# One plan slot sooner and the last store on another queue: attention products of a fused kernel on one core

## Chip, cores, metric

One Trainium2 chip, one core of it. The metric is device time in microseconds (us), the median of several executions. Executions can fall into a slower state, at a lower granted TensorE clock. Times inside a trace are us from the start of the profiled execution's span.

## The reference

A block-wise linear attention with decay (batch 4, 8 heads, 768 tokens, head width 64), followed by a bilinear feed-forward layer over 3072 tokens of width 512:

```python
for b in range(nb):                        # blocks of a sequence
    intra = np.einsum('bhic,bhjc->bhij', qb, kb) * Dmask[None]
    intra = np.einsum('bhij,bhjd->bhid', intra, vb)
    inter = np.einsum('bhid,bhde->bhie', qb * lam_pow[None], kv_state)
    out[:, :, sl] = intra + inter
    kv_state = lam_block[None, :, None, None] * kv_state + np.einsum('bhsd,bhse->bhde', kb_dec, vb)
...
a = x @ w_a; b = x @ w_b                   # 3072x512 by 512x1536
return (a * b @ w_out).astype(np.float32)
```

## The kernel before

Tokens come in 24 units of 128; the feed-forward layer runs over groups of units (`GROUPS = (4, 1, 2, 4, 4, 4, 4, 1)`). While a group's feed-forward products keep TensorE busy, a fixed plan slips the attention work of later units between them. A plan entry is (slot, piece, unit), where a slot is a place after one step of the group's products; entries with the same slot run in the order of the list.

```python
PLAN = {
    0: [(0, "V", 3), (8, "C", 0), ... (30, "PV", 4), (34, "O", 4),        # cut
        (35, "PK", 5), (35, "PV", 5)],
    ...
    2: [(0, "V", 6), (1, "T", 7), (1, "P", 8), (4, "T", 8), (4, "P", 9), (6, "S", 7),
        (6, "S", 8), (7, "V", 7), (6, "P", 10), (10, "V", 8), ...],       # cut
}
```

Pieces: O are a unit's attention products with the cast of their result to xT (ACT); S are scores (TensorE) and two mask products (VectorE, L330); V is the state update: `kvd` products on TensorE (L369), then a copy of the state on VectorE (L401), for which the next unit's `kvd` must wait, because they add to the same bank; P prepares a unit: two scaling products on GpSimd (L262 for k, L267 for q) and a cast of v to bf16 (L276).

```python
def prep_v(u):
    make_vb(u, "pool" if u < n0 + 3 else "dve")     # n0 = 4: from unit 7 on VectorE
    pump()                                           # issues the next loads
def kv_copy(u, ps, eng="dve"):
    ...
    nc.vector.tensor_mul(st..., ps..., bdiag_bc)     # L401; ps is a PSUM bank
...
def store(row, op, lo, hi):
    if row < g_u0[KEEP_GROUPS]:
        ...                                          # o_kept: ACT copy now, stored later
        return
    o_sb = o_pool.tile([128, d_model], F32, name="o_sb", tag="osb")
    nc.scalar.copy(o_sb[:, lo:hi], op[:, lo:hi])                       # L467
    nc.sync.dma_start(out=out_r[row][:, lo:hi], in_=o_sb[:, lo:hi])    # L468
...
            if last and t == n - 1:                  # the last unit, in three column parts
                for lo, hi in ((0, 256), (256, 384), (384, 512)):
                    ...
                    store(u0 + t, op, lo, hi)
```

Of the kernel before, what the change touches and what calls it, by code (L numbers as in the profile page):

```python
# [22 lines left out]
def _bc(ap, dims):  # L23
# [17 lines left out]

PLAN = {
    0: [(0, "V", 3), (8, "C", 0), (9, "C", 1), (15, "C", 2), (18, "C", 3), (23, "PK", 4),
        (26, "C", 4), (26, "T", 4), (29, "C", 5), (29, "S", 4), (30, "PV", 4), (34, "O", 4),
        (35, "PK", 5), (35, "PV", 5)],
    1: [(0, "V", 4), (2, "T", 5), (3, "PK", 6), (6, "PV", 6), (6, "S", 5), (7, "T", 6),
        (10, "S", 6), (12, "O2", (5, 6)), (13, "P", 7)],
# [18 lines left out]
def kernel(  # L66
# [11 lines left out]
    nc = tc.nc  # L78
    B, H, S, D = q.shape
# [3 lines left out]
    d_model, d_ff = moe_w_a.shape  # L83
# [25 lines left out]
    def ps_bank(name, shape, dt, hold=False, ffn=False, at=None):  # L109
        i = bank["next"] if at is None else at  # L110
        while i in bank["held"] or (ffn and i == bank["ffn"]):
            i = (i + 1) % 7
        if ffn:
            bank["ffn"] = i
        bank["next"] = (i + 1) % 7
        if hold:
            bank["held"].add(i)
        return ps_pool.tile(shape, dt, name=name, tag=f"ps{i}")
# [34 lines left out]
    def cast_w(kind, c, eng):  # L153
        t = staged.pop((kind, c))
        if kind == "o":
            dst = wo_sb[:, 2 * c:2 * c + 2, :]
        else:
            dst = (wa_sb if kind == "a" else wb_sb)[:, :, w_off[c]:w_off[c + 1]]
        if eng == "act":
            nc.scalar.copy(dst, t)  # L160
        elif eng == "pool":
            nc.gpsimd.tensor_copy(dst[:, :, :128], t[:, :, :128])
            nc.gpsimd.tensor_copy(dst[:, :, 128:], t[:, :, 128:])
        else:
            nc.vector.tensor_copy(dst, t)  # L165
        pump()
# [39 lines left out]
    for w, src in (("q", q), ("k", k)):  # L206
        x4_r = src[0, :, 0:PACK * BLK, :].rearrange("h (p r) d -> p h (r d)", r=PACK)
        n_h = 4 if w == "q" else 2
        for h in range(0, H, n_h):
            t = wst_pool.tile([128, 1024], F32, name=w + "4", tag="wst")[:, :n_h * 256]  # L210
            nc.sync.dma_start(out=t.rearrange("p (h x) -> p h x", h=n_h), in_=x4_r[:, h:h + n_h])
            t = t.rearrange("p (h r d) -> p h r d", h=n_h, r=PACK)
# [220 lines left out]
    out_r = out.rearrange("(t p) n -> t p n", p=128)  # L433
# [10 lines left out]
    def a_part(f, xT, gt, cuts=None):  # L444
        ps = half(wa_sb, f, xT, gt, "a_ps", cuts)
        a_sb = a_pool.tile([128, 512], BF16, name="a_sb", tag="a")
        nc.scalar.copy(a_sb[:, :gt], ps[:, :gt])  # L447
        return a_sb

    def b_part(f, xT, gt, a_sb, ab):  # L450
        ps = half(wb_sb, f, xT, gt, "b_ps")
        nc.vector.tensor_mul(ab[:, f, :gt], a_sb[:, :gt], ps[:, :gt])  # L452
# [4 lines left out]
        row, o_sb = kept.pop(0)  # L457
        nc.sync.dma_start(out=out_r[row], in_=o_sb)

    def store(row, op, lo, hi):  # L460
        if row < g_u0[KEEP_GROUPS]:
            o_sb = wst_pool.tile([128, 1024], F32, name="o_kept", tag="wst")[:, :d_model]
            nc.scalar.copy(o_sb, op)
            kept.append((row, o_sb))
            return
        o_sb = o_pool.tile([128, d_model], F32, name="o_sb", tag="osb")
        nc.scalar.copy(o_sb[:, lo:hi], op[:, lo:hi])  # L467
        nc.sync.dma_start(out=out_r[row][:, lo:hi], in_=o_sb[:, lo:hi])  # L468

    def out_mms(op, ab, t, fs, lo=0, hi=d_model):  # L470
        for f in fs:
            nc.tensor.matmul(op[:, lo:hi], lhsT=ab[:, f, t * 128:(t + 1) * 128],  # L472
                             rhs=wo_sb[:, f, lo:hi], start=(f == 0), stop=(f == FC - 1))

    def ffn(u0, n, xT, hook, first, last):
        gt = n * BLK
        ab = ab_pool.tile([128, FC, 512], BF16, name="ab", tag="ab")
        if first:
            for i, cs in enumerate(W_STEPS):
                nxt = W_STEPS[i + 1][0] if i + 1 < len(W_STEPS) else None  # L480
                fs = range(w_off[cs[0]] // 128, w_off[cs[-1] + 1] // 128)
                a_sbs = [a_part(f, xT, gt, ((0, gt - BLK), (gt - BLK, gt)) if f == 0 else None)
                         for f in fs]
                if i == 0:
                    cast_w("b", cs[1], "act")
                elif nxt:
                    cast_w("a", nxt, "dve")
                for n_f, (f, a_sb) in enumerate(zip(fs, a_sbs)):
                    b_part(f, xT, gt, a_sb, ab)
                    hook(f)  # L490
                    if i == 0 and n_f == 1:
                        cast_w("a", nxt, "dve")
                if nxt:
                    cast_w("b", nxt, "act")
            ops = [ps_bank("op", [128, d_model], F32, hold=True) for _ in range(n)]
            slot = FC
            for c in range(FC // 2):
                for t in range(n):
                    out_mms(ops[t], ab, t, range(2 * c, 2 * c + 2))
                    if c == FC // 2 - 1:  # L500
                        store(u0 + t, ops[t], 0, d_model)
                    hook(slot)
                    slot += 1
            bank["held"].clear()
            return
        for f in range(FC):
            a_sb = a_part(f, xT, gt)
            b_part(f, xT, gt, a_sb, ab)
            hook(f)
        for t in range(n):  # L510
            op = ps_bank("op", [128, d_model], F32, ffn=True)
            if last and t == n - 1:
                for lo, hi in ((0, 256), (256, 384), (384, 512)):
                    if lo:
                        op = ps_bank("op", [128, d_model], F32, ffn=True)
                    out_mms(op, ab, t, range(FC), lo, hi)
                    store(u0 + t, op, lo, hi)
                return
            out_mms(op, ab, t, range(FC // 2))
            hook(FC + 2 * t)  # L520
            out_mms(op, ab, t, range(FC // 2, FC))
            store(u0 + t, op, 0, d_model)
            hook(FC + 2 * t + 1)
# [135 lines left out]
    for g, n in enumerate(GROUPS):  # L659
# [6 lines left out]
        def hook(slot, plan=plan):  # L666
            for name, us in plan.get(slot, ()):
                if name == "C":
                    cast_w("o", us, "dve")
                elif name == "PK":  # L670
                    prep_k(us)
                elif name == "PV":
                    prep_v(us)
                elif name == "P":
                    prep_k(us)
                    prep_v(us)
                elif name == "W":
                    store_kept()
                elif name == "T":
                    piece_T(us)  # L680
                elif name == "S":
                    piece_S(us)
                elif name == "V":
                    piece_V(us)
                elif name == "O":
                    pieces_O((us,))
                elif name == "O2":
                    pieces_O(us)
                else:
                    pieces_O(us[:2], us[2:])  # L690

        ffn(g_u0[g], n, gx.pop(g), hook, g == 0, g + 1 == len(GROUPS))

# [28 lines left out]
```

## Time and profile before

| | before |
|---|---|
| time, first 3 runs | 233.46 us (233.22 to 233.78) |
| span of the profiled run | 231.5 us |
| TensorE / VectorE / ACT / GpSimd busy | 97% / 50% / 39% / 22% of the span |
| loss of TensorE's stream before the second group's first product | 0.34 us |
| end of the last ACT copy to the end of the span | 3.08 us |

TensorE is the bound: an engine other than TensorE matters only where TensorE waits for it. The prediction shows the lines for the first group's end and for the tail. From the timeline of the kernel before (start, length, engine, line, what):

```profile
69.91 2.48 DVE L330 TENSOR_TENSOR m<-kq,lotri 128x512 bf16<-128x512 f32 x4
...
72.30 0.41 DVE L276 CAST vb<-vf 128x512 bf16<-128x512 f32 x1
...
72.40 1.21 POOL L262 TENSOR_TENSOR qk<-kf,lp_k 128x512 bf16<-128x512 f32 x1 [2.37 <-DMA kf<-in_k_dram]
...
72.63 0.41 DVE L452 TENSOR_TENSOR ab<-a_sb,b_ps 128x256 bf16<-128x256 bf16 x1
...
72.97 0.68 DVE L401 TENSOR_TENSOR st<-kvd,bdiag 128x512 bf16<-128x512 f32 x1
...
73.70 0.38 PE L369 MATMUL kvd<-vb,qk 128*128 128x128 bf16 x4
```

VectorE works without a pause here: four mask products, the cast of unit 10's v, an `ab` product, the state copy. TensorE's `kvd` starts 0.05 us after that copy ends (72.97 + 0.68 = 73.65). That is no slack: in e1 and e11 below, where TensorE did wait for the copy, `kvd` also starts 0.05 us after its end. GpSimd's product for unit 11 starts when its load has landed, in this run at 72.40, after the cast had begun.

### The profile page before, as it was taken

Reading aid. Unit: us, or ns where it says so; the run is one execution under the profiler, and the core shown is the slowest. Engines: PE = TensorE matmul, PEld = TensorE weight load, DVE = VectorE, ACT = ScalarE, POOL = GpSimd, SP = SyncE. Lnnn points to the kernel's source line nnn. Section 1 sums busy time; section 2 is a strip of 40 time slices with the busy share of each in tenths; the row PEclk is TensorE's granted clock in tenths of the full one; section 3 lists DMA queues with packets and bytes.
Section 4 is the critical chain, followed back from the end, with each engine's and each line's share of the span. In section 5 each row is a group of like instructions: output and inputs, shape, how many; then the busy total and the mean of one; then the engine's idle time right before and its main releaser. Section 6 shows DMA issues by size and latency. Waiting matters only on the chain.

```text
span 231.5 us, 4532 instructions
## 1 busy us (share of the span) xinstructions
PE 225.1 (97%) x1779; PEld 124.8 (54%) x1779; DVE 115.9 (50%) x204; ACT 90.9 (39%) x172; POOL 50.8 (22%) x65
## 2 busy tenths in 40 slices
PE   7799999999999999999999999999999999999994
PEld 2484444459688654554544454544554544444493
DVE  0894757536469726676334584334483313331050
ACT  3677563066473243342233333233333234332261
POOL 6071000336564333334301533001200000000000
PEclk9999999999999999999999999999999999999999
DMA  4999999998999999999869995239300220000311
GB/s 154 303 281 349 349 364 301 299 189 189 204 229 161 225 195 217 213 184 213 304 201 203 218 175 113 93 103 194 66 3 0 91 93 0 1 0 23 115 45 50
DMA packets 96422, 38.84 MB, mean 168 GB/s; under 512 B 83344, under 2 KB 91920, under 8 KB 96400
## 3 DMA queue, kind: packets, MB, share of 16 engines
q1 hardware_dynamic: 96256, 38.54, 72.5%
q8 instruction: 14, 0.23, 0.4%
q14 instruction: 8, 0.07, 0.1%
q10 hardware_dynamic: 144, 0.00, 0.0%
HBM read 28.32 MB, written 6.29 MB: 149 GB/s over the span
## 4 chain that ended last, share of the span: by engine, by line
PE 87%; DMA 4%; SPq 3%; ACT 2%; DVE 1%; issue 0%
PE a_ps L439 27%; PE b_ps L439 26%; PE op L472 23%; PE o_ps L355 3%; DMA q<-in_q_dram 3%; PE kq L313 2%; SPq L129 2%; PE o_ps L345 2%; DMA qf<-in_q_dram 2%; PE kvd L369 2%; ACT scratch L565 1%; PE tps L299 1%; SPq L145 1%; DVE scratch L542 1%; PE kq L590 1%; ACT xT L362 0%
## 5 line engine op out<-in xcount | busy, mean ns | idle before, releaser
L452 DVE TENSOR_TENSOR ab<-a_sb,b_ps 128x512 bf16<-128x512 bf16 (+2 forms) x96 | 52.3, 552 | 78.4 <-PE b_ps L439 57.4
L439 PE MATMUL a_ps<-xT,wa_sb 128*128 128x512 bf16 (+3 forms) x388 | 77.0, 324 | 0.4 <-ACT xT L362 0.4
L439 PE MATMUL b_ps<-xT,wb_sb 128*128 128x512 bf16 (+2 forms) x384 | 77.1, 326 | 0.0
L447 ACT CAST a_sb<-a_ps 128x512 bf16<-128x512 f32 (+2 forms) x96 | 45.6, 481 | 62.6 <-PE a_ps L439 61.3
L472 PE MATMUL op<-wo_sb,ab 128*128 128x512 bf16 (+2 forms) x312 | 65.6, 363 | 0.0
L439 PEld LDWEIGHTS <-wb_sb 128*128 128x128 bf16 x384 | 34.5, 98 | 28.6 <-DVE wb_sb L165 0.3
L439 PEld LDWEIGHTS <-wa_sb 128*128 128x128 bf16 x388 | 34.0, 98 | 28.7 <-issue 0.8
L472 PEld LDWEIGHTS <-ab 128*128 128x128 bf16 x312 | 28.7, 98 | 29.9
L330 DVE TENSOR_TENSOR m<-kq,lotri 128x512 bf16<-128x512 f32 x47 | 29.3, 682 | 17.8 <-PE kq L313 17.2
L262 POOL TENSOR_TENSOR qk<-kf,lp_k 128x512 bf16<-128x512 f32 x18 | 19.3, 1074 | 74.8 <-DMA kf<-in_k_dram 58.2
L267 POOL TENSOR_TENSOR qk<-qf,lp_q 128x512 bf16<-128x512 f32 x20 | 21.9, 1095 | 23.3 <-DMA qf<-in_q_dram 23.3
L467 ACT COPY o_sb<-op 128x512 f32<-128x512 f32 (+2 forms) x19 | 10.3, 541 | 34.0 <-PE op L472 34.0
L362 ACT CAST xT<-o_ps 128x512 bf16<-128x512 f32 x22 | 12.0, 590 | 18.0 <-PE o_ps L355 17.5
L401 DVE TENSOR_TENSOR st<-kvd,bdiag 128x512 bf16<-128x512 f32 x18 | 12.3, 682 | 4.2 <-PE kvd L369 3.6
L276 DVE CAST vb<-vf 128x512 bf16<-128x512 f32 x17 | 9.7, 570 | 0.0
L301 ACT COPY qkT<-tps 128x1024 bf16<-128x1024 bf16 x5 | 5.1, 1012 | 9.9 <-PE tps L299 9.9
L198 PE MATMUL idle<-idle_sb 128*128 128x128 bf16 (+1 forms) x31 | 6.8, 359 | 1.3 <-DVE idle_sb L193 1.3
L355 PE MATMUL o_ps<-m,vb 128*64 128x128 bf16 x192 | 7.8, 222 | 0.0
L276 POOL CAST vb<-vf 128x512 bf16<-128x512 f32 x7 | 4.4, 631 | 13.1 <-DMA vf<-in_v_dram 13.1
L345 PEld LDWEIGHTS <-st 128*128 128x128 bf16 x80 | 5.4, 98 | 2.8
L313 PE MATMUL kq<-qkT 64*128 64x128 bf16 x160 | 6.6, 218 | 0.0
L355 PEld LDWEIGHTS <-vb 128*64 128x64 bf16 x192 | 5.7, 109 | 1.4
(57 smaller groups left out, 86.5 us busy)
## 6 DMA issues: line engine op xcount, KB each, us to landing
vf<-in_v_dram SPq DMA_DIRECT2D x24, 256.0 KB, 4.9
qf<-in_q_dram SPq DMA_DIRECT2D x20, 256.0 KB, 4.6
kf<-in_k_dram SPq DMA_DIRECT2D x20, 256.0 KB, 4.7
out_dram<-o_sb SPq DMA_DIRECT2D x16, 256.0 KB, 2.0
wst<-in_moe_w_a_dram SPq DMA_DIRECT2D x6, 512.0 KB, 8.6
wst<-in_moe_w_b_dram SPq DMA_DIRECT2D x6, 512.0 KB, 8.7
wst<-in_moe_w_out_dram SPq DMA_DIRECT2D x6, 512.0 KB, 8.6
out_dram<-o_kept SPq DMA_DIRECT2D x7, 256.0 KB, 2.5
```

The lines of the kernel that those rows point to most:

```text
L262: eng_of(eng).tensor_mul(qk[:, 1], raw.pop((u, "k")), lp_k[:, u % NB].to_broadcast([128, H, D]))
L267: eng_of(eng).tensor_mul(U[u]["qk"][:, 0], raw.pop((u, "q")), lp_q[:, u % NB].to_broadcast([128, H, D]))
L276: eng_of(eng).tensor_copy(vb, vf)
L313: nc.tensor.matmul(kq[i][:, hp, :], lhsT=d["kT"][p, hp, :], rhs=d["qT"][p, hp, :], start=True, stop=True, skip_group_check=True)
L330: nc.vector.tensor_mul(m, kq[i], lotri_bc)
L355: nc.tensor.matmul(d["o"][p, hp, :], lhsT=d["vb"][:, 2 * hp + i, :], rhs=d["m"](i, hp), start=(first and hp == 0), stop=True, skip_group_c ...
L362: nc.scalar.copy(xT[:, :, col:col + BLK], o_ps)
L401: nc.vector.tensor_mul(st[:].rearrange("p hp i d -> p hp (i d)"), ps[:].rearrange("p hp i d -> p hp (i d)"), bdiag_bc)
L439: nc.tensor.matmul(ps[:, lo:hi], lhsT=w_sb[:, s, f * 128:(f + 1) * 128], rhs=xT[:, s, lo:hi], start=(s == 0), stop=(s == KS - 1), skip_gro ...
L447: nc.scalar.copy(a_sb[:, :gt], ps[:, :gt])
L452: nc.vector.tensor_mul(ab[:, f, :gt], a_sb[:, :gt], ps[:, :gt])
L472: nc.tensor.matmul(op[:, lo:hi], lhsT=ab[:, f, t * 128:(t + 1) * 128], rhs=wo_sb[:, f, lo:hi], start=(f == 0), stop=(f == FC - 1))
```

## The change

Its intent: close TensorE's wait of 0.34 us at the end of the first group by issuing unit 4's products one slot sooner, and let ACT, which writes the last output tile, issue its store itself, so that no other engine has to see ACT's signal.

```diff
-        (26, "C", 4), (26, "T", 4), (29, "C", 5), (29, "S", 4), (30, "PV", 4), (34, "O", 4),
+        (26, "C", 4), (26, "T", 4), (29, "C", 5), (29, "S", 4), (30, "PV", 4), (33, "O", 4),
...
-    def store(row, op, lo, hi):
+    def store(row, op, lo, hi, queue=None):
...
-        nc.sync.dma_start(out=out_r[row][:, lo:hi], in_=o_sb[:, lo:hi])
+        (queue or nc.sync).dma_start(out=out_r[row][:, lo:hi], in_=o_sb[:, lo:hi])
...
-                    store(u0 + t, op, lo, hi)
+                    store(u0 + t, op, lo, hi, nc.scalar if hi == d_model else None)
```

## The prediction

> **What bounds the kernel now.** The kernel before took 233.22 to 233.78 us in three runs, median 233.46; the profiled execution's span is 231.5 us. I read first the page's busy shares and its chain of waits, then the list of who waited on TensorE, then the timeline of the two places that the change touches.
>
> ```profile
> PE 225.1 (97%) x1779; PEld 124.8 (54%) x1779; DVE 115.9 (50%) x204; ACT 90.9 (39%) x172; POOL 50.8 (22%) x65
> ...
> PE 87%; DMA 4%; SPq 3%; ACT 2%; DVE 1%; issue 0%
> ```
>
> TensorE is busy in 97% of the span and carries 87% of the chain that ends last. So only two sorts of change can shorten this kernel without removing matmuls: closing a gap in TensorE's stream, or shortening the head or the tail in which TensorE does nothing. The change tries one of each. The list of TensorE's waits shows how few gaps there are:
>
> ```profile
> PE idle L198 <- DVE idle_sb L193: 1.3, 1, 1.3
> PE tq L554 <- DVE scratch L542: 1.1, 4, 0.5
> PE a_ps L439 <- ACT xT L362: 0.4, 2, 0.2
> PE tn L574 <- ACT scratch L565: 0.2, 1, 0.2
> ```
>
> The columns are total us, times, longest. The third line is the one that the plan's new slot can touch: the first product of a group waits for ACT's copy of the attention result into xT. One of its two waits is at 17.9 us (first group, untouched), the other is at 51.23 us, between the first and the second group. The timeline there (start, length, engine, line, what):
>
> ```profile
> 48.50 1.46 PE L472 MATMUL op<-wo_sb,ab 128*128 128x512 bf16 x6
> ...
> 49.13 1.56 ACT L463 COPY o_kept<-op 128x512 f32<-128x512 f32 x3 [2.01 <-PE op L472]
> ...
> 49.79 0.39 PE L345 MATMUL o_ps<-qkT,st 128*128 128x128 bf16 x4
> ...
> 50.11 0.41 PE L355 MATMUL o_ps<-m,vb 128*64 128x128 bf16 x8
> ...
> 50.46 0.61 PE L472 MATMUL op<-wo_sb,ab 128*128 128x512 bf16 x2
> 50.57 0.62 ACT L362 CAST xT<-o_ps 128x512 bf16<-128x512 f32 x1
> ...
> 51.15 0.59 ACT L463 COPY o_kept<-op 128x512 f32<-128x512 f32 x1
> 51.23 0.38 PE L439 MATMUL a_ps<-xT,wa_sb 128*128 128x128 bf16 x4 [0.17 <-ACT xT L362]
> ```
>
> Unit 4's products (L345, L355) stand before the last pair of output products (L472 at 50.46). ACT's cast to xT starts at 50.57, just after they end, and lasts 0.62 us, to 51.19; the first a_ps starts 0.04 us later. The one pair at 50.46 does not cover that cast. The page's idle of 0.17 us is counted from the modelled end of the pair (51.07). The stream itself stopped earlier: two 512-wide matmuls at 0.216 us each (the six at 48.50 take 1.46 us, of which the last occupies 0.38: five steps of 0.216) end their issue at 50.46 + 0.43 = 50.89. TensorE's real loss is 51.23 - 50.89 = 0.34 us.
>
> The tail, from the timeline and from the queue's own waits:
>
> ```profile
> 226.84 0.37 ACT L467 COPY o_sb<-op 128x256 f32<-128x256 f32 x1 [1.27 <-PE op L472]
> 227.24 1.56 SPq L468 DMA_DIRECT2D out_dram<-o_sb  x3
> 227.51 0.27 ACT L467 COPY o_sb<-op 128x128 f32<-128x128 f32 x1 [0.30 <-PE op L472]
> 228.18 0.27 ACT L467 COPY o_sb<-op 128x128 f32<-128x128 f32 x1 [0.40 <-PE op L472]
> ```
>
> ```profile
> SPq L468 <- ACT o_sb L467: 6.5, 3, 6.0
> SPq L717 <- DMA out_dram<-o_sb: 1.2, 1, 1.2
> ```
>
> Each store has its own copy before it. The last copy ends at 228.45. The three issues run from 227.24 to 228.80, each 0.33 us (the line's own figures are 332 to 333 ns), so the last begins at 228.47, some 0.02 us after its copy. The one before it began at about 227.81 and was over at 228.14: SP was idle for a third of a microsecond before the last store. It waited for ACT's data, not for a free queue. After the issue nothing runs until the data has landed (1.6 us from the start of the issue), and the closing barrier takes the last 1.4 us.
>
> **What the Trainium skill says.** "DMA: Bandwidth & Descriptors", section "Issuing engines are not separate DMA queues", says that issuing from several engines saves only the sequencer's own issue time, as all transfers run on the same 16 DMA engines. The trace agrees as far as it goes: the issue is 0.33 us and SP has it free. "Perfetto Trace Analysis", section "DMA Instruction — HWDGE (DVE, Sync)", says that the profiled DMA instruction starts when its semaphores are satisfied and ends when the sequencer is free, without the data movement: hence 0.33 us beside 1.6 us to landing here. The same page, "Tensor Engine Instruction (MATMUL, LD_WEIGHTS)", says that a matmul's end is estimated, which is why I count from starts. "TensorE: Matmul & The Clock Gate", section "Step-by-step: what each phase is for", gives about 216 ns between back-to-back 512-wide matmuls; this trace has 0.216.
>
> **The change, part by part.** No instruction is added or dropped but one event wait on SP. On TensorE the 12 products of unit 4 move ahead of one pair of output products; on ACT the cast to xT moves ahead of the third o_kept copy; one 64 KB store goes from SP's list to ACT's.
>
> *Unit 4 one slot sooner.* The pair that is overtaken is 2 x 0.216 = 0.43 us, so unit 4's products start at 49.79 - 0.43 = 49.36 and end 0.43 sooner, at about 50.11 instead of 50.54. Their inputs allow it: the second mask product is done at 48.34 + 0.68 = 49.02, before the L355 products at 49.68. On ACT the first two o_kept copies start at 49.13 and 49.61 (three take 1.56 us, a step of 0.48), so ACT is free at 50.09 and the cast can run at 50.13. It ends at 50.75, a_ps may go at 50.79, and TensorE is busy with the two pairs until 50.89 as before. The wait of 0.34 us is gone with 0.1 us to spare. The third o_kept copy then starts at about 50.67, ends at 51.27, and the bank it frees is wanted by the third a_ps only, at about 52.0. The fourth stays at 51.15.
>
> Does the 0.34 survive? ACT is full until 51.65, so the first a_sb cast stays where it is, and DVE, with the state update behind it, catches up two products later. I read the waits that TensorE meets in group 1, where products are 128 wide and slack is small. Most hang on ACT and DVE work that itself follows TensorE and moves with it. One does not: unit 6's transposes at 55.91 need POOL's work, which ends at 54.49 + 1.04 = 55.53 and starts from a load's landing. Moved by 0.34 they would start at 55.57: it fits by hundredths. Afterwards no TensorE wait has POOL or a DMA close behind. I take 0.30 us (0.15 to 0.34).
>
> *The last store from ACT.* It still waits for the same copy's write and still takes its 0.33 us issue and its landing. The other ACT-issued transfer in the trace, lam at 0.80 us, took 0.41 us to issue beside SP's 0.45 at the same moment: no sign that one queue is quicker. After landing SP goes through the same five waits in the same order and the same barrier. Worth 0.0 us, give or take 0.15.
>
> Sum: 233.46 - 0.30 - 0.00 = 233.16; I say 233.15.
>
> **The rivals.** (1) *The wait is moved, not removed.* POOL's load-bound work at 55.53, or ACT's backlog, takes the 0.34 back within group 1. For it: the slack of hundredths, and ACT without a pause from 49.13 to 51.9. Against: banks and a_sb buffers are free in time by the sums above. Time 233.4 to 233.5. (2) *ACT's issue is quicker at the end,* since no other engine's sequencer has to see ACT's signal. Against: SP begins only 0.02 us after the copy. At most 0.1 us more: 233.05. (3) *ACT's queue is slower,* because it was last used at 0.8 us, or because the sequencer that copies must also issue. For it: nothing in the trace but that 0.41 against 0.33 us (a different transfer). Time 233.25 to 233.4. (4) *A bound elsewhere:* the tail alone decides, and a gain at 51 us is lost later to a load. Against: after 62 us TensorE's stream shows no wait that a load ends.
>
> **Range and chances.** The runs of before differ by 0.56 us, more than the gain. I add that scatter (some 0.25 us each way around the median) to the range of the sum (-0.1 to -0.5): 232.8 to 233.55. A change of 2% is 4.7 us; both parts together touch 0.34 us of waiting and one issue of 0.33. So almost surely within 2%.
>
> **What would show it right or wrong.** In the profile after, the a_ps wait on xT should be one time, 0.2 us in total, a_ps of group 1 should start at 50.9 instead of 51.23, and the last ACT copy should begin at about 227.85 instead of 228.18. Then 0.02 us to an issue on ACT's queue, about 1.6 us to landing, and 3.0 us from the last copy's end to the span's end as now. If unit 6's transposes wait for POOL, rival 1 holds; if the tail is not 3.0 us, the store's move has an effect that I deny. The prediction fails if the time leaves 232.8 to 233.55 in fast runs.

## The result, and the profile after

| | before | after |
|---|---|---|
| median of 5 runs | 233.46 us (233.22 to 233.78) | 233.71 us (233.40 to 234.35) |
| ratio | | 1.0012, 95% interval 0.9993 to 1.0031 |
| profiled span | 231.53 us | 231.85 us |

A ratio here is the mean time of one kernel's fast runs over that of the other's of the same rounds, so not quite the ratio of the medians quoted. 233.71 us is outside the predicted 232.8 to 233.55: the 0.30 us did not come, and the profiled span is 0.32 us longer.

From the page of the kernel after, busy shares and the chain of waits:

```profile
PE 225.6 (97%) x1779; PEld 124.8 (54%) x1779; DVE 116.1 (50%) x204; ACT 90.8 (39%) x172; POOL 50.7 (22%) x65
...
PE 91%; DMA 3%; DVE 2%; ACT 2%; issue 1%; SPq 0%; DVEq 0%
```

The same work in the same counts. VectorE's share of the chain has gone from 1% to 2%. Who TensorE waited for in the kernel after (total us, times, longest):

```profile
PE tq L554 <- DVE scratch L542: 0.6, 3, 0.2
PE kvd L369 <- DVE st L401: 0.4, 1, 0.4
PE a_ps L439 <- ACT xT L362: 0.2, 1, 0.2
```

The wait for xT is one instead of two, as intended. But there is a line that before did not have: `kvd` waits for VectorE's state copy. Both places in the timeline of the kernel after; first the end of the first group:

```profile
49.18 1.07 ACT L463 COPY o_kept<-op 128x512 f32<-128x512 f32 x2 [2.02 <-PE op L472]
...
49.41 0.39 PE L345 MATMUL o_ps<-qkT,st 128*128 128x128 bf16 x4
...
50.08 1.04 PE L472 MATMUL op<-wo_sb,ab 128*128 128x512 bf16 x4
50.19 0.58 ACT L362 CAST xT<-o_ps 128x512 bf16<-128x512 f32 x1
...
50.95 0.39 PE L439 MATMUL a_ps<-xT,wa_sb 128*128 128x128 bf16 x4
```

The first `a_ps` starts at 50.95 instead of 51.23, in a trace whose work runs 0.05 us later up to here (the o_kept copies start at 49.18 instead of 49.13): 0.33 us are won. Then unit 8's state products (`kvd`), which follow VectorE's copy of unit 7's state:

```profile
70.62 1.04 POOL L262 TENSOR_TENSOR qk<-kf,lp_k 128x512 bf16<-128x512 f32 x1 [1.32 <-DMA kf<-in_k_dram]
...
71.62 1.04 POOL L267 TENSOR_TENSOR qk<-qf,lp_q 128x512 bf16<-128x512 f32 x1
...
72.02 0.92 DVE L276 CAST vb<-vf 128x512 bf16<-128x512 f32 x1
...
72.86 0.41 DVE L452 TENSOR_TENSOR ab<-a_sb,b_ps 128x256 bf16<-128x256 bf16 x1
...
73.20 0.68 DVE L401 TENSOR_TENSOR st<-kvd,bdiag 128x512 bf16<-128x512 f32 x1
...
73.93 0.38 PE L369 MATMUL kvd<-vb,qk 128*128 128x128 bf16 x4 [0.37 <-DVE st L401]
```

The cast starts 0.28 us sooner than before, at 72.02, but lasts 0.92 us instead of 0.41: it stands beside GpSimd's product, which ends at 72.66, and is over 0.28 us after that. All that follows on VectorE is late by as much, and TensorE starts `kvd` at 73.93, 0.23 us later than before instead of 0.28 sooner: 0.51 us are lost. The chain that ended last shows the handover (start, length, what), first before:

```profile
73.40 0.44 PE b_ps L439 x4
73.84 0.24 PE kvd L369 x4
74.08 0.44 PE a_ps L439 x4
```

and after:

```profile
72.02 0.72 DVE vb L276
72.74 0.12 issue
72.86 0.41 DVE ab L452
73.27 0.61 DVE st L401
73.88 0.04 issue
73.93 0.38 PE kvd L369 x4
```

Before, the chain stays on TensorE. After, it comes from VectorE's cast: what shortens TensorE's work ahead of this point no longer counts, what ends GpSimd's product does.

The tail, from the timeline of the kernel after:

```profile
228.41 0.27 ACT L467 COPY o_sb<-op 128x128 f32<-128x128 f32 x1 [0.41 <-PE op L472]
...
228.70 0.35 ACTq L468 DMA_DIRECT2D out_dram<-o_sb  x1
```

From the end of that copy to the end of the span (the tail, from here on) 3.18 us pass, before 3.08. The sum of the two traces: -0.33 (slot) + 0.51 (`kvd`) + 0.10 (tail) + 0.05 (the later head) = +0.33, against 231.85 - 231.53 = +0.32.

### The profile page after: what moved, and what is told of

It reads as the page before. It is cut to its first block, busy times and chain, and to the rows that moved or that the text cites. A ratio compares the mean times of both kernels' runs of the same rounds, so it can differ in the third digit from the quotient of the medians.

```text
span 231.9 us, 4531 instructions
## 1 busy us (share of the span) xinstructions
PE 225.6 (97%) x1779; PEld 124.8 (54%) x1779; DVE 116.1 (50%) x204; ACT 90.8 (39%) x172; POOL 50.7 (22%) x65
## 4 chain that ended last, share of the span: by engine, by line
PE 91%; DMA 3%; DVE 2%; ACT 2%; issue 1%; SPq 0%; DVEq 0%
PE op L472 27%; PE a_ps L439 26%; PE b_ps L439 26%; PE o_ps L355 3%; DMA q<-in_q_dram 3%; PE kq L313 2%; PE o_ps L345 2%; PE kvd L369 2%; ACT scratch L565 1%; PE tps L299 1%; DVE m L330 1%; DVE scratch L542 1%; PE kq L590 1%; DVE ab L452 0%; PE kv L369 0%
## 5 line engine op out<-in xcount | busy, mean ns | idle before, releaser
L301 ACT COPY qkT<-tps 128x1024 bf16<-128x1024 bf16 x5 | 5.1, 1012 | 9.9 <-PE tps L299 9.9
L198 PE MATMUL idle<-idle_sb 128*128 128x128 bf16 (+1 forms) x31 | 7.3, 378 | 1.3 <-DVE idle_sb L193 1.3
```

## The experiments

The theory formed on these traces: VectorE's cast of unit 10 and GpSimd's products for unit 11 cannot go on at the same time. The end of GpSimd's work is set by the loads (in all fourteen traces its k product for unit 11 starts 0.16 us after that unit's k has landed, also where the view puts the wait down to TensorE), so the slot moves VectorE and TensorE ahead into it and gains nothing. The rivals: the store's queue is what costs; the collision is a freak of one trace; or the slot costs something elsewhere. Each expectation carries the letters under which its theories stood when it was written. All runs gave right results. Times of before are those measured together with the run. None differs by 2%, so the argument rests on instants inside the traces.

Each trace gives a few instants, all counted from the start of ACT's copy of unit 4's q and k (`qkT<-tps`, L301), which starts 46.1 to 48.5 us after the span's start and so takes out the scatter of the head. They are worked out from the traces' records and rounded to 0.01 us; the slot moves the first `a_ps` from 5.130 to 4.795, called 0.33 us here:

| trace | last store, slot | first a_ps | GpSimd's q product ends | cast of unit 10: start, length | kvd of unit 8 starts |
|---|---|---|---|---|---|
| before | SP, 34 | 5.13 | 28.51 | 26.20, 0.41 | 27.59 |
| e11_before_again | SP, 34 | 5.13 | 26.37 | 26.20, 0.46 | 27.64 |
| e10_before_sp_four_more | SP, 34 | 5.13 | 26.87 | 26.19, 0.95 | 28.13 |
| e2_store_only | ACT, 34 | 5.13 | 25.10 | 26.20, 0.41 | 27.59 |
| e4_state_early | SP, 34 | 5.13 | 26.59 | 26.80, 0.42 | 27.57 |
| after | ACT, 33 | 4.79 | 26.51 | 25.86, 0.92 | 27.77 |
| e8_changed_again | ACT, 33 | 4.79 | 26.37 | 25.86, 0.79 | 27.63 |
| e1_slot_only | SP, 33 | 4.79 | 26.27 | 25.86, 0.69 | 27.54 |
| e3_both_state_early | ACT, 33 | 4.79 | 25.91 | 26.46, 0.42 | 27.23 |
| e5_slot_state_early | SP, 33 | 4.79 | 27.87 | 26.46, 0.51 | 27.23 |
| e6_cast10_gpsimd | ACT, 33 | 4.79 | 26.15 | none on VectorE | 27.23 |
| e7_slot_casts_gpsimd | SP, 33 | 4.79 | 26.89 | none on VectorE | 27.23 |
| e9_both_casts_gpsimd | ACT, 33 | 4.79 | 26.41 | none on VectorE | 27.23 |
| e12_casts_gpsimd | SP, 34 | 5.13 | 26.87 | none on VectorE | 27.57 |

What happens at this `kvd` lasts to the end: from its start to the end of the last ACT copy 154.75 to 154.77 us pass in twelve of the fourteen traces. Only e4 and e10 lose more on the way (155.14 and 155.18), each with a cast of 1.06 or 1.10 us near 80 us.

GpSimd's k product comes right before its q product, and each takes 1.04 us when nothing holds it up. In the trace of before both came late: the k product started at 26.30, after the cast had begun, so the cast did not stand behind it. In e5 the cast stood behind the k product only.

### e1_slot_only, e2_store_only: each part alone

e1 changes 34 to 33 in `PLAN[0]` and leaves the store; e2 changes the store and leaves the plan.

> Unit 4's products one slot sooner, the last store still on SP. Theory A (the slot's gain of 0.33 us at 51 us is real, and is taken back at about 74 us when the cast of unit 10's values on VectorE collides with GpSimd's work and so delays the state update that TensorE waits for): TensorE's gap before the first a_ps of group 1 is under 0.05 us instead of 0.33. If the cast collides (lasts 0.9 us instead of 0.42) there is a gap of about 0.5 us before kvd near 73.9 us and the time is 0 to 0.2 us above before; if it does not, the gap there is under 0.05 us and the time is 0.3 us below before. Theory B (the ACT store costs the time): 0.3 us below before in any case.

> The last store on ACT, unit 4 at its old slot. Theory A: TensorE's stream as in before (gap 0.33 us at 51.2 us), time within 0.15 us of before. Theory B (the ACT store costs the time): from the end of the last ACT copy to the end of the span 3.5 us or more instead of 3.08, and the time 0.4 us or more above before. The profile of the changed kernel had 3.18 us there, so a small cost of 0.1 us is expected by both.

Measured: e1 233.45 us, ratio 0.9993 (0.9979 to 1.0006); e2 233.72 us, ratio 1.0021 (0.9995 to 1.0047); before 233.50. e1's time, 0.05 us below before, decides nothing (0 to 0.2 us above was expected with a collision). In its trace e1 has `a_ps` at 4.79, a long cast (0.69; 0.9 was expected) and `kvd` at 27.54, only 0.05 sooner than before: with the slot alone the collision is there, and it eats the gain. From the timeline of e1:

```profile
71.54 1.04 POOL L267 TENSOR_TENSOR qk<-qf,lp_q 128x512 bf16<-128x512 f32 x1
...
72.17 0.69 DVE L276 CAST vb<-vf 128x512 bf16<-128x512 f32 x1
...
73.12 0.68 DVE L401 TENSOR_TENSOR st<-kvd,bdiag 128x512 bf16<-128x512 f32 x1
...
73.85 0.38 PE L369 MATMUL kvd<-vb,qk 128*128 128x128 bf16 x4
```

e2 has neither (`a_ps` 5.13, cast 0.41); its time is 0.22 us above before, more than the 0.15 expected and not resolved by its ratio. The tail follows the store: 3.06 us in e1, 3.17 in e2. e2's profiled run was one of those in which the head came some 2 us late (235.67 us); instants counted from the copy are not touched by that.

### e3_both_state_early, e4_state_early: the state copy ahead of the cast

e3 is the kernel after with one entry of the plan moved; e4 is the kernel before with the same edit. Unit 7's state update goes ahead of the cast in VectorE's order, so unit 8's `kvd` no longer stands behind it:

```diff
-        (6, "S", 8), (7, "V", 7), (6, "P", 10), (10, "V", 8),
+        (6, "S", 8), (6, "V", 7), (6, "P", 10), (10, "V", 8),
```

> The changed kernel, with the state update of unit 7 moved ahead of the preparation of unit 10 in group 2, so that its VectorE work stands before the cast that can collide. Theory A: no gap before kvd near 74 us whatever the cast lasts, the 0.33 us of the slot stays to the end, and the time is 0.2 to 0.4 us below before, so 0.4 to 0.6 us below the changed kernel. Theory B: the time stays at that of the changed kernel, 0.2 us above before.

> The kernel before with only that state update moved. Theory A: the kernel before meets the collision in some of its runs, where it costs less because TensorE comes 0.33 us later: time 0 to 0.2 us below before. Theory B: no effect, within 0.1 us.

Measured: e3 233.38 us, ratio 0.9992 (0.9979 to 1.0005), so 0.12 us below before where 0.2 to 0.4 was expected; e4 233.76 us, ratio 1.0007 (0.9989 to 1.0024); before 233.50. In e3 `kvd` starts at 27.23, 0.36 sooner than before's 27.59, so the 0.33 of the slot survives once the cast is out of its way (its tail, with ACT's store, is 0.09 us longer than before's). Its cast met no GpSimd product; e5's did. e4 itself was no gain (0 to 0.2 us was expected): its trace has no wait for VectorE at this `kvd` (27.57), but a later cast at 79.61 lasts 1.06 us beside a GpSimd product from 79.34 to 80.38, and TensorE is 0.36 us later from 81.2 on. Other casts can be hit as well.

### e5_slot_state_early: the same without the store

e5 is e3 with SP's store as before.

> Slot 33 and the earlier state update, last store on SP. Theory A (slot gains 0.33 us, the collision at 73 us takes it back unless the state update goes first; the ACT store costs 0.10 us in the tail): from the last TensorE signal to the end 3.36 us, as in the runs with SP's store, against 3.46 with ACT's; no gap before the state products; time 0.1 us below the same kernel with ACT's store (233.38), so 0.25 to 0.35 us below before. Theory C (the tail difference is chance): 3.46 us in about half of such runs, no difference from 233.38.

Measured: 233.35 us, ratio 0.9982 (0.9964 to 0.9999), before 233.69. `kvd` at 27.23, tail 3.06 us (the 3.36 and 3.46 of the expectations count from TensorE's last signal, some 0.3 us before the last copy's end). In this trace GpSimd came late: its k product ran from 25.64 to 26.69, the cast began at 26.46 and ended at 26.97, 0.28 after it, and GpSimd's q product, begun in the meantime at 26.65, took 1.22 us instead of 1.04. Each is held up by the other, and with the state copy ahead of the cast TensorE notices nothing.

### e6_cast10_gpsimd, e7_slot_casts_gpsimd: the cast taken off VectorE

e6 is the kernel after with unit 10's cast on GpSimd (`or u == 10`); e7 is before with slot 33 and the casts of all units under 13 on GpSimd, where they follow its own products and cannot run beside them:

```diff
-        make_vb(u, "pool" if u < n0 + 3 else "dve")
+        make_vb(u, "pool" if u < 13 else "dve")
```

> The changed kernel with one edit: the cast of unit 10's values runs on GpSimd itself instead of on VectorE, so that it cannot be held up by GpSimd's work; order of everything else kept. Theory A: the wait before kvd at 73.9 us (0.51 us in the changed kernel) is under 0.05 us, the 0.33 us of the slot is kept until there, the time is 0.2 us below before and 0.4 us below the changed kernel, the tail remains 3.46 us. Rival D (the state update is late for another reason than that cast): the gap of 0.3 to 0.5 us stays.

> Slot 33, last store on SP, and the value casts of units 7 to 12 all on GpSimd. Theory A: no cast on VectorE in groups 1 and 2, so no collision and no new TensorE gap between 51 and 82 us; tail 3.36 us; time 0.3 us below before, and a smaller spread of runs than the 0.6 us of before. Against it: GpSimd has 0.6 us more per unit and may delay the transposes; then a gap stands before the transposes or DMA transposes near 64 to 85 us.

Measured: e6 233.09 us, ratio 0.9978 (0.9949 to 1.0006); e7 232.57 us, ratio 0.9957 (0.9935 to 0.9978), the lowest time; before 233.69. In e6 `kvd` is at 27.23, as in e7: with that one cast gone the gap is gone, against rival D. The timeline of e7:

```profile
71.94 1.05 POOL L267 TENSOR_TENSOR qk<-qf,lp_q 128x512 bf16<-128x512 f32 x1
71.95 0.41 DVE L452 TENSOR_TENSOR ab<-a_sb,b_ps 128x256 bf16<-128x256 bf16 x1
...
72.28 0.68 DVE L401 TENSOR_TENSOR st<-kvd,bdiag 128x512 bf16<-128x512 f32 x1
...
73.33 0.39 PE L369 MATMUL kvd<-vb,qk 128*128 128x128 bf16 x4
```

GpSimd's product ends late in this run (72.99), and nothing comes of it: the `ab` product and the state copy beside it keep their 0.41 and 0.68 us, the copy is done 0.37 us before `kvd` starts. It is the cast that GpSimd holds up, not VectorE's other work. One thing I had not expected: the tail of e7 is 2.69 us, 0.37 shorter than in e1 with the same store. Of e7's gain of about 1.1 us so much has nothing to do with the collision; with the 0.36 at `kvd` that makes 0.73, and the rest the traces do not show. e6's tail, 2.76 us, was shorter than expected as well.

### e8_changed_again: is it one trace?

e8 is the changed kernel once more.

> The changed kernel once more, on this chip beside the others. Theory A: the slot's gap stays closed; a gap before kvd near 73.9 us as long as the cast lasts beyond its 0.42 us undisturbed (up to 0.5 us), tail 3.46 us; time 0.1 us above before (-0.1 to +0.3).

Measured: 233.94 us, ratio 1.0015 (0.9990 to 1.0039), before 233.69. The cast lasts 0.79 us, `kvd` is at 27.63, 0.40 later than without a collision. So the collision is in all three traces that have slot 33 and the cast in its old place on VectorE.

### e9_both_casts_gpsimd, e10_before_sp_four_more: the tail

The tails of e6 and e7 asked for an explanation. In the list of SP's instructions (counted in the traces' records; no view of the profile prints it) there is an odd place near the end: SP stands still for 0.34 to 0.37 us ahead of its 208th recorded instruction, whatever that is. (A pause like it, 0.44 us, stands in all fourteen traces ahead of the 80th, 128 places earlier.) What comes there depends on how many instructions the kernel gave SP before:

| trace | last store | recorded SP instructions | the 208th is | landing to end | last copy to end |
|---|---|---|---|---|---|
| before | SP | 213 | the fifth of the five closing waits | 1.401 | 3.078 |
| e1_slot_only | SP | 213 | the same | 1.385 | 3.056 |
| after | ACT | 211 | the second drain, in the closing barrier | 1.471 | 3.182 |
| e2_store_only | ACT | 211 | the same | 1.466 | 3.168 |
| e6_cast10_gpsimd | ACT | 210 | a wait of the closing barrier | 1.051 | 2.758 |
| e7_slot_casts_gpsimd | SP | 208 | the last one, where SP waits for the barrier anyway | 1.017 | 2.692 |
| e9_both_casts_gpsimd | ACT | 206 | there is none | 1.002 | 2.715 |
| e10_before_sp_four_more | SP | 217 | the first of the five closing waits | 0.976 | 2.569 |

e9 and e10 were made to test this: e9 is the kernel after with e7's casts, which takes more of SP's waits away; e10 is the kernel before with four stores in two halves each, which puts SP instructions in:

```diff
+        if row in (16, 17, 18, 20):
+            for c in (0, 256):
+                nc.sync.dma_start(out=out_r[row][:, c:c + 256], in_=o_sb[:, c:c + 256])
+            return
```

> The changed kernel (slot 33, last store on ACT) with the value casts of units 7 to 12 on GpSimd, that is e7 with ACT's store. In the traces so far SP pauses 0.3 us before its 208th recorded instruction; before the change that is a wait after the landing, after the change a drain of the closing barrier, in e7 it is the last instruction of all and costs nothing. Theory A1 (of the store's 0.10 us, 0.03 are ACT's slower issue and landing and 0.07 the moved pause): tail from the end of the last copy to the end of the span 2.72 us against e7's 2.69, time 232.6. Theory A2 (an ACT store costs 0.10 us by itself): 2.79 us, 232.7.

> The kernel before, with four of the stores in the middle of the run cut in two, which adds four instructions to SP's list and puts its 208th at the first closing wait, where SP has to wait for the landing anyway. If the pause sits at a place in the list: from landing to the end 1.02 to 1.08 us instead of 1.40, tail 2.70 instead of 3.07, time 0.36 us below before. If the pause belongs to the fifth closing wait itself: tail 3.07 and the time that of before.

Measured: e9 232.86 us, ratio 0.9968 (0.9937 to 0.9998); e10 233.27 us, ratio 0.9984 (0.9956 to 1.0012); before 233.58. In e10 the pause fell between the last store's issue and the first wait, where SP has to wait for the data anyway, and the tail lost half a microsecond with more to issue (2.569 us, where 2.70 was expected; its last store also landed 0.08 us sooner after its issue than before's). e9 against e7 is the store's own price, without the pause in either tail: 2.715 - 2.692 = 0.02 us, as theory A1 had it (2.72, where A2 had 2.79). ACT's issue takes 353 ns where SP's takes 332, and starts 21 ns after the signal instead of 17.

e10 showed another thing, unasked. Its plan is that of before, and yet the cast is long, as its timeline shows:

```profile
72.28 1.04 POOL L267 TENSOR_TENSOR qk<-qf,lp_q 128x512 bf16<-128x512 f32 x1
72.65 0.95 DVE L276 CAST vb<-vf 128x512 bf16<-128x512 f32 x1
```

and from its list of TensorE's waits:

```profile
PE kvd L369 <- DVE st L401: 0.4, 1, 0.4
```

The collision is no property of the new slot. Here GpSimd's product ended at 26.87 after the copy, and so the cast of before's plan, at 26.19, was caught too.

### e11_before_again, e12_casts_gpsimd: before once more, and e7 without the slot

e11 is the kernel before, e12 the kernel before with e7's edit of `make_vb` alone.

> The kernel before once more, for a second profile. Theory A: first a_ps of group 1 again 5.12 us after the transposed copy at 46.1 us (4.79 with slot 33). Unit 10's cast begins 26.19 us after it; if GpSimd's work for unit 11 overlaps it, the cast ends late and the state products come up to 0.3 us later than 27.59; if not, at 27.59. Tail 3.06 to 3.08 us.

> The kernel before (slot 34, SP's store) with the value casts of units 7 to 12 on GpSimd: e7 without the slot. Theory A: with the collision out of the way the slot is worth its whole 0.33 us, so this kernel is at 232.9 where e7 is at 232.57; state products of unit 8 at 27.56 us after the transposed copy against 27.23. Rival (the slot's gain is lost in any case): 232.6.

Measured: e11 233.54 us, ratio 1.0000 (0.9967 to 1.0034), which says how little a ratio can resolve (0.3% is 0.8 us); e12 233.05 us, ratio 0.9967 (0.9944 to 0.9991); before 233.58. e11's cast was just touched (0.46 us, `kvd` 27.64), and its tail is 3.07 us. e12 against e7 is the slot with no cast on VectorE to be hit: `kvd` at 27.57 against 27.23, a gain of 0.34 us in the traces. The medians differ by 0.48 us, the ratios by 0.0010, some 0.23 us, so this agrees with 0.33 and does not prove it. e12's own gain over before is not the collision: its `kvd` is only 0.02 us sooner than before's, but its tail is 2.70 us, 0.38 shorter: the moved casts also took five instructions out of SP's list, so that its 208th is the last one, as in e7.

### What the traces say together

In the five traces in which the cast stands behind GpSimd's q product (after, e1, e8, e10, e11), the cast ends 0.28 us after that product (once 0.29; e5 has 0.28 behind the k product), and `kvd` follows the cast's end by 0.98 to 0.99 us. So with a collision `kvd` starts 1.26 us after GpSimd's product ends, whichever slot is planned: 26.51 + 1.26 = 27.77 for after (27.77 measured), 26.27 + 1.26 = 27.53 for e1 (27.54), 28.13 for e10 (28.13). Without one it starts at 27.57 to 27.59 with slot 34 and at 27.23 with slot 33. e8 and e11 are a matched pair by chance: slot 33 and slot 34, GpSimd's product ends at 26.37 in both, and `kvd` starts at 27.63 and 27.64. So slot 33 keeps its 0.33 us only where GpSimd's product ends before 27.23 - 1.26 = 25.97 (or comes after the cast), keeps a part up to 27.59 - 1.26 = 26.33, and keeps nothing from there on. In ten of the fourteen traces taken the product ended between 26.15 and 26.90, mostly past that.

## Why the prediction was wrong, step by step

**The slot closes the wait at the first group's end: right.** The wait for xT is one, `a_ps` starts 0.33 us sooner (4.79 instead of 5.13 after the copy in every trace), the cast to xT ends before the two pairs do.

**"Does the 0.34 survive?": this is the step that failed,** in its sentence "Afterwards no TensorE wait has POOL or a DMA close behind". I had looked for GpSimd as the direct releaser of a TensorE wait. It stood one link further back: `kvd` waits for the state copy, that for the cast in VectorE's order, that for GpSimd, and GpSimd's end for a load. The timeline of before shows this `kvd` 0.05 us behind the copy, so with no slack; I took the copy for work that "itself follows TensorE and moves with it". It does until it meets a load-bound neighbour. In place of the 0.30 us credited, the trace after shows +0.18 at `kvd` (27.77 against 27.59): -0.33 of the slot, +0.51 of the collision. There was a sign of it beforehand: on the page of before VectorE's 17 casts average 570 ns where one alone takes 0.42 us, and in its trace the cast at 64.65 lasts 1.00 us and also ends 0.28 us after a GpSimd product.

**Unit 6's transposes: right, with luck.** In the kernel after they did not wait for GpSimd, but its work for unit 6 ended 1.3 us sooner than before, at 54.19, so the fit "by hundredths" was never put to the test.

**Rival 1, "the wait is moved, not removed": right in kind, wrong in place.** I gave it 233.4 to 233.5 us and put it into group 1, where it did not happen; it was at 74 us, in group 2.

**The store is worth 0.0, and the tail stays 3.0 us: right that nothing is gained, wrong in size.** The last copy, forecast for 227.85, began at 228.41: the slot's gain had not come through. The tail is 0.10 us longer (3.18 against 3.08; 3.17 in e2 against 3.06 in e1). About 0.02 us are ACT's slower issue (rival 3), as e9 against e7 shows. The rest lies after the landing, and goes with SP's pause, which by two instructions fewer in SP's list fell into the closing barrier instead of ahead of it. I had written that SP goes through "the same five waits in the same order and the same barrier"; the list was shorter. Of the 0.56 us between 233.15 and 233.71, the trace gives 0.30 (gain not kept) + 0.18 (the collision costs more than the gain in this trace) + 0.10 (tail) = 0.58; that this meets a difference of medians so closely is partly chance, as single runs scatter by as much. What the slot costs on average over many runs I cannot say: the landing of this load varies by a microsecond between most traces and by 3 us in all, and the profiled run of before was a lucky one, with its load about 2 us later than in most.

**Rival 4, a bound elsewhere:** partly. A load does decide later, through two engines.

**The range:** it is narrower than its own terms. Slot 0.15 to 0.34, store 0.15 either way and scatter 0.25, added end to end, reach from 232.72 to 233.71, not from 232.8 to 233.55.

What stays open: why SP pauses there, and why the loads' timing differs so much between executions of one kernel.

## What to carry to other kernels

Before crediting a closed gap, follow the chain of every later wait with small slack back over all its links, and stop only at something that moves with the change or at something that does not, such as a load: two instructions of VectorE and GpSimd that only just miss each other are such a meeting point. A gain of a tenth of a per cent in one stage is kept only if the next tight point is loosened with it. Here that is to take the cast off VectorE (e7, 232.57 us, the lowest time), though 0.39 us of its lead over before lie in the shorter tail, and e12 has that too. And where times scatter by more than the effect, counting instants of several traces from one common event decides what a ratio cannot.

## What the Trainium skill lacked or had wrong

- "SBUF — State Buffer", section "Who interferes with whom", says that VectorE's copies and casts in a two-port mode and GpSimd take a shared pair of ports as an exclusive lock, that whichever issues first keeps it for the whole instruction, and that a VectorE instruction outside these modes with at most one input in SBUF is not concerned. The traces agree: unit 10's cast takes 0.41 us alone and up to 0.95 behind GpSimd, the second one waits in either order (GpSimd's product 1.22 us instead of 1.04 in e5), and the four mask products with one input in PSUM take 2.48 us whether GpSimd runs beside them (after, e10) or not (before). I had not looked it up before predicting, as the change touches no GpSimd instruction. What the page lacks is the remainder: a blocked cast of unit 10 ended 0.28 us after GpSimd's product, not its full 0.41.
- "DMA: Bandwidth & Descriptors", section "Issuing engines are not separate DMA queues": the trace agrees that another queue moves no data sooner (1.65 us from issue to landing on SP, 1.68 on ACT). It has no figure for an issue by engine: the issue took 332 ns on SP and 353 on ACT.
- No page has the pause of 0.34 to 0.37 us in SP ahead of its 208th recorded instruction (nor the 0.44 us ahead of its 80th). The first is worth 0.4 to 0.5 us of a tail, according to where it falls. Only its place in the list is shown, not its cause.
